# First-stage units and chunk units of a fused Fourier filter and feed-forward kernel, planned at other steps

## The chip, the cores and the metric

The kernel runs on one core of one Trainium2 chip. The metric is the device time of one execution in microseconds; the median of several executions is compared. Engines are named as in the profile: PE is TensorE's matmul, PEld its weight load, DVE is VectorE, ACT ScalarE, POOL GpSimd, SP the engine whose queue issues most DMAs.

## The reference

The input x has 8 batches of 3008 tokens with 256 channels. Each channel of each batch is filtered along the tokens in the frequency domain, and the result goes through a feed-forward layer with a hard-swish. All is fp32.

```python
X = np.fft.rfft(x, axis=1)                      # x: (8, 3008, 256)
y = np.fft.irfft(X * F[None], n=3008, axis=1)   # F = filt_r + 1j * filt_i, (1505, 256)
h = y.reshape(24064, 256) @ w_in                # w_in: (256, 2048)
g = h * np.clip(h + 3.0, 0.0, 6.0) / 6.0
out = g @ w_out                                 # w_out: (2048, 256)
```

## The kernel before

**The feed-forward is the main loop.** The 24064 tokens are 47 blocks of 512 (index k), and the 2048 hidden columns are 8 parts of 256 (index p). One step of the loop is one pair (k, p), numbered 8k + p. It multiplies up with w_in (`up_1` to `up_5`, L570, into the PSUM tiles `al` and `be`), applies the hard-swish on ACT and DVE (L615, L620), and multiplies down the part before it with w_out (`down`, L646, into four PSUM banks `po`). Both products use seven half-size products each in place of eight (Strassen's scheme), with the sums on DVE (L627 to L630) and, for the up side, on POOL (`t_sums`, L563). The sums of a finished block are added up, and its output stored, in the first two steps of the block after (`out_1` to `out_5`, stores on SP at L723).

**The Fourier filter of later batches is planned into the steps of the loop.** 3008 is 47 x 64, and the transform is split accordingly. For one batch it is a chain of units:

- `a_unit` (L385), eight per batch, the first stage: 16 matmuls from four loaded columns of x (ring `xs` of three) into two PSUM banks of the pool `psF`. ACT evicts the first bank into a tile of `t1p` (L388), and `a_sums` on DVE (L394, L395) combines it with the second bank, which is read straight from PSUM and stays taken until then. `z_store` (L402) writes the tile to HBM with four DMAs on POOL's queue. `x_load` (L322) loads the columns on SP.
- `t2_load`, `b_unit` (L428), `f_unit` (L449 to L451), `y_unit` (L459, L460): the second stage and the filter itself.
- `bi_unit` (L471), six per batch, the first inverse stage: four products into two banks of `psF`, both evicted by ACT (L474), then `g_store` on POOL's queue (L491).
- `t4_load` (L517, on SP) and `n_unit` (L524), the last inverse stage: each chunk of up to five columns of 94 tokens has two halves, dh = 0 and dh = 1, each with one bank of `psF` and an eviction by ACT into `xn` (L530), the feed-forward's input. The half that completes a block starts `t_sums`.

The pool `psF` has two banks, and all of these units share them. The pool `t1p` has two tiles.

**What sets the order.** A dictionary `plan` maps a step to functions, filled by `at(step, fn, ...)`. Functions listed in `EARLY` (`a_unit`, `b_unit`, `bi_unit`, `n_unit`) run in a step right after `up_1`, so their matmuls stand behind its three products on PE; all others run at the end of the step. Within a step they run in the order in which they were planned: chunk units first, then batch by batch. The queues of all engines are in program order.

For batch index n from 2 to 7 `places(n)` gives the steps. With `first[n]` the first block that holds tokens of the batch (0, 5, 11, 17, 23, 29, 35, 41), the eight first-stage units stand in the two blocks from step 8 x first[n] - 56 on, here called the batch's window; "+1" is the window's second step. The inverse units of a batch stand at 8 x first[n] - 40 + 16r + (8, 14, 17) for r = 0 and 1. The chunk units stand by a table `N_AT` of kinds of block, one letter for each block of the window and the four that follow; its entries are the steps of the two halves for a chunk that is alone in its block, for the first of two and for the second of two. A chunk that begins a batch and is alone in its block has both halves at +6.

```python
for n in range(2, B):
    for d, kind in enumerate("aaABAB"):
        kinds[first[n] - 7 + d] = kind
...
if c >= 3:
    at(max(a_at[c - 3], s - 6), x_load, n, c)
```

Of the kernel before, what the change touches and what calls it, by code (L numbers as in the profile page):

```python
# [33 lines left out]
B = 8  # L34
# [11 lines left out]
NP = DFF // 256  # L46
# [90 lines left out]
def kernel(  # L137
# [365 lines left out]
    def token(i):  # L503
        b, j, n = chunks[i]
        return b * N + j * TOK, n * TOK
# [230 lines left out]
    with tc.manual_schedule():  # L736
# [112 lines left out]
        n_at = {0: -2, 1: -2}  # L849
        kinds = {}  # L850
        for n in range(2, B):
            for d, kind in enumerate("aaABAB"):
                kinds[first[n] - 7 + d] = kind

        N_AT = {"a": ((2, 4), (2, 4), (6, 6)), "A": ((4, 5), (1, 1), (4, 5)), "B": ((2, 3), (1, 1), (2, 3))}
        N_FIRST = {0: ((3, 4),), 1: ((), (2, 2), (3, 3)), 2: ((1, 1),), 3: ((1, 1),)}
        in_block = {}
        for i in range(2, len(chunks)):
# [2 lines left out]
        for i in range(2, len(chunks)):  # L861
            k = token(i)[0] // BLK
            head = chunks[i][1] == 0
            same = in_block[k]
            steps = (N_FIRST.get(k - 1) or N_AT[kinds.get(k - 1, "a")])[same.index(i) + 1 if len(same) > 1 else 0]
            if head and len(same) == 1:
# [12 lines left out]
        def places(n):  # L879
            if n == 1:  # L880
                return (list(range(2, NB + 2)), [12, 13, 15, 18, 19, 20, 22, 23, 26, 27, 28, 30],
                        [14, 15, 16, 19, 21, 22, 24, 25, 27, 29, 30, 31], [16, 21, 24, 29, 31, 32])
            k = first[n] * NP
            a_at = [k - 7 * NP + i for i in (1, 3, 5, 7, 9, 11, 13, 15)]
            f_at, y_at, bi_at = ([k - (5 - 2 * r) * NP + i for r in range(2) for i in p]
                                 for p in ((2, 3, 6, 7, 12, 13), (4, 5, 10, 11, 14, 15), (8, 14, 17)))
            return a_at, f_at, y_at, bi_at

        prev = None
        for n in range(1, B):  # L890
            a_at, f_at, y_at, bi_at = places(n)
            for c, s in enumerate(a_at):
                at(s, a_unit, n, c)
                if n > 1:
                    at(s, a_sums, n, c)
                at(s, z_store, n, c, nc.sync if n == 1 else nc.gpsimd)
                if c >= 3:
                    at(max(a_at[c - 3], s - 6), x_load, n, c)
                elif n > 1:
                    at(max(prev[c + NB - 3], s - 6), x_load, n, c)  # L900
            for c in range(NT):
                s = f_at[2 * (c - TB) + (n == 1)] + 1 if c >= TB else a_at[-1] + 1
                at(s, t2_load, n, c)
                s = f_at[2 * (c - FB) + 1] + 1 if c >= FB else a_at[-1 if n > 1 else 3] + 1
                at(s, table_load, n, c)
            for i in range(NU):
                if i % 2 == 0 or n == 1:
                    at(f_at[i], b_unit, n, i)
                if i % 2 == 0:
                    at(bi_at[i // 2], bi_unit, n, i)  # L910
                    at(bi_at[i // 2], g_store, n, i)
                at(y_at[i], y_unit, n, i)
            for i in range(NU):
                at(f_at[i], f_unit, n, i)
            prev = a_at
# [4 lines left out]
        for i in range(len(items) + 1):  # L920
            up = i < len(items)
            k, p = items[min(i, len(items) - 1)]
# [54 lines left out]
        k, v, add = NBLK - 1, nc.vector.tensor_tensor, ALU.add  # L977
# [37 lines left out]
```

## Time and profile before

The five runs have a median of 2712.89 us (2712.3 to 2714.12). The profiled execution took 2712.89 us, with a span of 2711.1 us from the first to the last recorded instruction.

| engine | busy us | instructions |
|---|---|---|
| ACT | 1308.1 | 2614 |
| POOL | 373.2 | 598 |
| DVE | 2022.8 | 3503 |

| group | busy us | one, ns |
|---|---|---|
| PE, down products, L646 | 1402.8 | 276 |
| PE, first stage, L385 | 65.0 | 389 |
| PE, inverse stage, L471 (batch index 1 to 7) | 51.8 | 614 |
| PE, last inverse stage, L524 | 124.5 | 272 |
| ACT, eviction of the inverse stage, L474 | 53.0 | 595 |
| ACT, eviction of the first stage, L388 | 37.5 | 598 |

A group is all instructions of one source line on one engine. Matmuls of fp32 appear as two instructions each. Their ends are modelled and they overlap, so the length of a step is read from the start of a matmul to the start of the same matmul one step later, not from busy times. A wait in the list of waits names the engine and line that waited, who released it, the total in microseconds, how often, and the longest. The chain of waits follows the last instruction back to what released it, step by step.

### The profile page before, as it was taken

How to read it: one execution, taken by the hardware profiler on the slowest of the kernel's cores; microseconds unless marked ns; L12 is line 12 of the kernel's file. 1: busy time of each engine (PE TensorE's matmuls, PEld its weight loads, DVE VectorE, ACT ScalarE, POOL GpSimd, SP SyncE). 2: the span in 40 equal slices, each digit the busy share in tenths (PEclk: the TensorE clock that was granted, in tenths of full speed). 3: DMA queues.
4: the chain of work that ended last, by engine and by line, in shares of the span. 5: the costliest groups of instructions: out<-in, count | busy, mean ns of one | idle time of the engine just before them, and what ended most of it. 6: DMA issues, size and time to landing. Idle time of an engine off the chain costs nothing.

```text
span 2711.1 us, 48871 instructions
## 1 busy us (share of the span) xinstructions
PE 2679.5 (99%) x18846; PEld 2368.8 (87%) x18846; DVE 2022.8 (75%) x3503; ACT 1308.1 (48%) x2614; POOL 373.2 (14%) x598
## 2 busy tenths in 40 slices
PE   9899999999999999999999999999999999999998
PEld 6588889888898888888898888888888988899997
DVE  7968867787677876787767877678776778766665
ACT  3344444444444444444454544445444454444443
POOL 2421111101110012100121011210112101000000
PEclk9999999999999999999999999999999999999999
DMA  8732133211332123321233112331123321110000
GB/s 234 206 104 72 50 87 93 73 35 45 86 96 70 35 50 93 90 63 36 51 98 90 55 38 53 94 90 55 37 55 93 90 58 36 42 31 17 18 9 16
DMA packets 106597, 185.88 MB, mean 69 GB/s; under 512 B 23609, under 2 KB 66297, under 8 KB 106049
## 3 DMA queue, kind: packets, MB, share of 16 engines
q1 hardware_dynamic: 88607, 138.05, 18.1%
q0 software_dynamic: 17152, 44.22, 6.2%
q8 instruction: 149, 2.44, 0.4%
q14 instruction: 83, 0.68, 0.1%
q10 hardware_dynamic: 606, 0.49, 0.1%
HBM read 110.74 MB, written 71.93 MB: 67 GB/s over the span
## 4 chain that ended last, share of the span: by engine, by line
PE 96%; DVE 3%; ACT 0%; DMA 0%; issue 0%; POOL 0%; POOLq 0%; DVEq 0%; SPq 0%
PE po L646 43%; PE al L570 24%; PE be L570 17%; PE psn L524 4%; PE psf L471 2%; PE psf L385 2%; PE psf L428 1%; PE po L352 1%; PE po L437 0%; PE psf L437 0%; DVE g L620 0%; DVE y L277 0%; DVE y L288 0%; DVE y L290 0%; DVE w_all L293 0%; PE al L779 0%
## 5 line engine op out<-in xcount | busy, mean ns | idle before, releaser
L646 PEld LDWEIGHTS po<-w_all,g 128*128 128x128 f32 x10304 | 1363.3, 191 | 145.4 <-issue 35.0
L646 PE MATMUL po<-w_all,g 128*128 128x128 f32 x10304 | 1402.8, 276 | 0.6 <-DVE g L620 0.6
L615 ACT ACTIVATE r<-h,half_c 128x512 f32<-128x512 f32 x736 | 531.3, 722 | 328.4 <-DVE h L596 316.4
L620 DVE SCALAR_TENSOR_TENSOR g<-r,h 128x512 f32<-128x512 f32 x736 | 506.6, 688 | 208.7 <-ACT r L615 194.4
L570 PE MATMUL al<-xt,w_all 128*128 128x256 f32 x2208 | 660.0, 381 | 1.2 <-DVE h L601 0.6
L570 PE MATMUL be<-xn,w_all 128*128 128x256 f32 x1472 | 437.8, 379 | 0.0
L596 DVE TENSOR_TENSOR h<-be,s 128x512 f32<-128x512 f32 x368 | 254.3, 691 | 224.2 <-PE be L570 213.4
L570 PEld LDWEIGHTS al<-xt,w_all 128*128 128x128 f32 x2208 | 335.2, 192 | 2.5 <-issue 1.3
L570 PEld LDWEIGHTS be<-xn,w_all 128*128 128x128 f32 x1472 | 279.7, 190 | 37.9
L610 ACT ACTIVATE h<-al 128x256 f32<-128x256 f32 x368 | 141.4, 384 | 344.2 <-PE al L570 344.2
L601 DVE TENSOR_TENSOR h<-al,s 128x256 f32<-128x256 f32 x368 | 156.2, 424 | 166.9 <-PE al L570 165.8
L628 DVE TENSOR_TENSOR g<-g 128x512 f32<-128x512 f32 x368 | 255.9, 695 | 12.6
L591 ACT ACTIVATE s<-al 128x256 f32<-128x256 f32 x368 | 141.4, 384 | 208.4 <-PE al L570 206.2
L582 ACT ACTIVATE s<-be 128x256 f32<-128x256 f32 x368 | 141.4, 384 | 176.3 <-PE be L570 176.3
L570 PE MATMUL al<-xn,w_all 128*128 128x256 f32 x736 | 219.9, 381 | 0.5 <-ACT h L610 0.5
L570 PE MATMUL be<-xt,w_all 128*128 128x256 f32 x736 | 218.9, 379 | 0.0
L630 DVE TENSOR_TENSOR g<-g 128x256 f32<-128x256 f32 x368 | 170.8, 464 | 12.5
L581 ACT ACTIVATE s<-al 128x256 f32<-128x256 f32 x368 | 141.4, 384 | 70.9 <-PE al L570 70.9
L627 DVE TENSOR_TENSOR g<-g 128x256 f32<-128x256 f32 x368 | 156.6, 426 | 12.6
L402 POOL DMA_DIRECT2D z_tmp<-t x192 | 95.5, 504 | 457.2 <-DVE t L395 447.1
L570 PEld LDWEIGHTS be<-xt,w_all 128*128 128x128 f32 x736 | 139.8, 190 | 18.9
L491 POOL DMA_DIRECT2D g_tmp<-t x84 | 52.9, 634 | 580.2 <-ACT t L474 580.2
(139 smaller groups left out, 1832.8 us busy)
## 6 DMA issues: line engine op xcount, KB each, us to landing
g_tmp<-t POOLq DMA_DIRECT2D x96, 256.0 KB, 3.7
t<-g_tmp SPq DMA_DIRECT2D x188, 120.0 KB
t<-z_tmp SPq DMA_DIRECT2D x42, 512.0 KB
z_tmp<-t POOLq DMA_DIRECT2D x192, 96.0 KB, 4.0
out_dram<-o SPq DMA_DIRECT2D x321, 47.0 KB
xs<-in_x_dram SPq DMA_DIRECT2D x112, 128.0 KB
ft<-in_filt_r_dram SPq DMA_DIRECT2D x168, 64.0 KB
ft<-in_filt_i_dram SPq DMA_DIRECT2D x168, 64.0 KB
```

The lines of the kernel that those rows point to most:

```text
L570: nc.tensor.matmul(ps, w_in[p][:, w, :], x, start=start, stop=stop, skip_group_check=True)
L581: nc.scalar.activation(out=s[:, 0, :], in_=al, func=AXT.Copy)
L582: nc.scalar.activation(out=s5, in_=be[:, 1, :], func=AXT.Copy)
L591: nc.scalar.activation(out=s[:, 1, :], in_=al, func=AXT.Copy)
L596: nc.vector.tensor_tensor(out=st["h"][0].rearrange("p (a n) -> p a n", a=2), in0=be, in1=s, op=ALU.add)
L601: nc.vector.tensor_tensor(out=st["h"][1][:, 256:512], in0=al, in1=s5, op=ALU.add)
L615: nc.scalar.activation(out=r, in_=st["h"][i], func=AXT.Relu, bias=half_c, scale=1.0 / 6.0)
L620: nc.vector.scalar_tensor_tensor(out=st["g", k, p][:, o:o + 2, :].rearrange("p a n -> p (a n)"), in0=st["r", i], scalar=1.0, in1=st["h"][i ...
L627: v.tensor_tensor(out=g[:, G1, :], in0=g[:, G3, :], in1=g[:, G22, :], op=ALU.add)
L628: v.tensor_tensor(out=g[:, G3:G2 + 1:2, :], in0=g[:, G3:G1 + 1, :], in1=g[:, G11:G11 + 1, :].broadcast_to([P, 2, 256]), op=ALU.subtract)
L630: v.tensor_tensor(out=g[:, G4, :], in0=g[:, G12, :], in1=g[:, G2, :], op=ALU.subtract)
L646: nc.tensor.matmul(st["po", k][bank][:, part, u, :], g[:, a, ts(u, P)], w_out[p][:, w, :], start=(p == 0 and n in OPENS and u == 0), stop= ...
```

## The change

Two lists of steps change. In the window's first block (new kind "c") a chunk that is alone has both halves at +6, the first of two chunks both halves at +3, and the second both at +6; before, that block was of kind "a". The eight first-stage units stand at +2, +4, +7, +9, +11, +13, +14 and +15 of the window; before, at +1, +3, and so on by twos to +15. What is planned relative to these (`a_sums`, `z_store`, `x_load`, `t4_load`) moves with them. The start of `t2_load`, one step after the last first-stage unit, stays.

```diff
         for n in range(2, B):
-            for d, kind in enumerate("aaABAB"):
+            for d, kind in enumerate("caABAB"):
                 kinds[first[n] - 7 + d] = kind
 
-        N_AT = {"a": ((2, 4), (2, 4), (6, 6)), "A": ((4, 5), (1, 1), (4, 5)), "B": ((2, 3), (1, 1), (2, 3))}
+        N_AT = {"c": ((6, 6), (3, 3), (6, 6)), "a": ((2, 4), (2, 4), (6, 6)), "A": ((4, 5), (1, 1), (4, 5)), "B": ((2, 3), (1, 1), (2, 3))}
...
             k = first[n] * NP
-            a_at = [k - 7 * NP + i for i in (1, 3, 5, 7, 9, 11, 13, 15)]
+            a_at = [k - 7 * NP + i for i in (2, 4, 7, 9, 11, 13, 14, 15)]
```

The units planned into the window of batch index 3 (steps 80 to 95; the halves of a chunk are written .0 and .1, with the number of its columns):

| step | before | after |
|---|---|---|
| +1 | last inverse unit of index 2, first-stage unit 0 | last inverse unit of index 2 |
| +2 | chunk of 2, .0 | first-stage 0 |
| +3 | first-stage 1 | chunk of 2, .0 and .1 |
| +4 | chunk of 2, .1 | first-stage 1 |
| +5 | first-stage 2 | |
| +6 | chunk of 5, .0 and .1 | chunk of 5, .0 and .1 |
| +7 | first-stage 3 | first-stage 2 |
| +9 | first-stage 4 | first-stage 3 |
| +10 | chunk of 5, .0 | chunk of 5, .0 |
| +11 | first-stage 5 | first-stage 4 |
| +12 | chunk of 5, .1 | chunk of 5, .1 |
| +13 | first-stage 6 | first-stage 5 |
| +14 | | first-stage 6 |
| +15 | first-stage 7 | first-stage 7 |

The windows of indices 4 to 6 have the same list. That of index 2 has a chunk of one column and no inverse unit at +1; that of index 7 has no chunk at +2 to +4.

## Prediction, made before the changed kernel ran

> **What bounds the kernel now.** I read the busy shares, the chain that ended last, the list of waits of PE, the chain in time order around one changed place, and last the busy time of the engines step by step. A step is one pass of the main loop (256 of the 2048 hidden columns for one block of 512 tokens, with whatever is planned into it); it starts with the first product of `up_1`, the matmul `al<-xn` that follows a run of `po`.
>
> ```profile
> PE 2679.5 (99%) x18846; PEld 2368.8 (87%) x18846; DVE 2022.8 (75%) x3503; ACT 1308.1 (48%) x2614; POOL 373.2 (14%) x598
> ...
> PE 96%; DVE 3%; ACT 0%; DMA 0%; issue 0%; POOL 0%; POOLq 0%; DVEq 0%; SPq 0%
> ```
>
> TensorE sets the end: 96% of the chain is its own work. Moving a planned unit to another step neither adds nor removes a matmul, so the change can only act on the few places where PE waits. The waits of PE name one group of them:
>
> ```profile
> PE psf L385 <- ACT t L474: 3.4, 5, 0.7
> ```
>
> Five times the first-stage unit (L385) waited for the evictions of an inverse unit (L474). L385 takes two PSUM banks of tag f, L471 takes two, and the pool has two. The chain in time order at the first of the five:
>
> ```profile
> 664.52 0.86 PE be L570 x4
> 665.38 1.03 PE psf L471 x8
> 666.41 0.02 issue
> 666.43 0.61 ACT t L474
> 667.04 0.04 issue
> 667.08 1.58 PE psf L385 x16
> 668.66 0.64 PE po L646 x4
> ...
> 681.60 1.02 PE psf L385 x16
> ```
>
> The reader is to see the 0.67 us between the two units, and that the sixteen L385 matmuls then take 1.58 us against 1.02 us at 681.60, since half of them need the second bank, whose eviction runs 0.6 us behind the first. The same step and three neighbours as windows (columns: stretch, length, busy time of PE, PEld, DVE, ACT, POOL, granted clock, DMA share and rate):
>
> ```profile
> 663.92:673.54 9.62, 8.94 (x68) 6.60 (x67) 6.10 (x14) 4.66 (x10) 1.92 (x3) 1.00 0.23 60
> 888.79:896.15 7.36, 7.36 (x52) 5.91 (x51) 5.42 (x12) 4.05 (x9) 1.93 (x3) 1.00 0.26 62
> 723.38:730.75 7.37, 7.37 (x61) 6.22 (x60) 6.04 (x14) 3.58 (x8) 0.73 (x1) 1.00 0.01 3
> 717.23:723.38 6.15, 6.15 (x45) 5.79 (x44) 4.83 (x9) 3.46 (x8) 2.00 (x4) 1.00 0.25 65
> ```
>
> In this order: inverse unit and first-stage unit in one step, inverse unit alone, first-stage unit alone, nothing. All have the full clock.
>
> **The change, part by part.** Its own time is 2712.89 us, span 2711.1, 1.8 us outside the span; the median of the runs is also 2712.89, so differences carry over as they are.
>
> *First unit from +1 to +2 of its window.* Step +1 keeps the inverse unit alone (7.36), the unit makes some other step 7.37 in place of 6.15. Before: 9.62 + 6.15 = 15.77. After: 7.36 + 7.37 = 14.73. The gain is 1.04 us a place. Places: the window of batch index n starts at step 8 x first[n] - 56; the batch ahead has its last inverse unit at 8 x first[n-1] - 24 + 17, and first grows by 6, so that is the window's +1 for n = 3 to 7. For n = 2 the batch ahead has its own list, whose last inverse unit is at step 32, one before that window's +1. So five, as the list of waits counts, not six: 5 x 1.04 = 5.2 us.
>
> Here a rule gives another sum. Taking PE's busy row as its work, the double step has 9.62 - 8.94 = 0.68 us idle, and five of them 3.4 us. The Trainium skill's page "Trainium Kernel Development and Optimization", section Performance Expectations, says matmul busy time is a bad measure of closeness to the limit, since matmuls are pipelined, and points to weight loads. The rows side with it: the L385 group counts 1.58 us as busy for work that takes 1.02. PEld idles 9.62 - 6.60 = 3.02 us there, against 1.15 to 1.45 in the two single steps. I take 5.2, and 3.4 as its lower end; no upper end beyond 6.2 (six places) is in sight.
>
> *The other units,* from 3, 5, 7, 9, 11, 13, 15 to 4, 7, 9, 11, 13, 14, 15. In the trace such a unit costs 7.37 - 6.15 = 1.22 us at every position, so moving it is nothing on PE, provided its resources are free. New are three units in consecutive steps (+13, +14, +15), six windows. The rows of such a stretch (unit at +13 in a step that starts at 752.64; nothing at +14 from 760.01; unit at +15 from 766.16):
>
> ```profile
> 759.65 0.69 DVE L395 TENSOR_TENSOR t<-t,psf 128x512 f32<-128x512 f32 x1
> 760.01 0.60 PE L570 MATMUL al<-xn,w_all 128*128 128x256 f32 x2
> 761.34 1.50 POOL L402 DMA_DIRECT2D z_tmp<-t  x3 [0.19 <-issue]
> 768.70 0.60 ACT L388 ACTIVATE t<-psf 128x512 f32<-128x512 f32 x1 [0.65 <-PE psf L385]
> ...
> L402 POOL DMA_DIRECT2D z_tmp<-t x4: 501/506/513, 760.6 to 762.3; - x4
> DMA to landing us min/median/max: 2.3/2.4/2.5
> ```
>
> (1) PSUM: the unit's second bank is held until its `a_sums` end, 760.34, which is 0.33 us into the next step. A unit's first matmul comes 1.39 us into its step (754.03 in a step from 752.64). Slack 1.06 us: no wait. DVE keeps up: a unit's step has 4.91 to 6.04 us of DVE work in 7.37. (2) The `t1` buffers: +15 writes the buffer of +13. That store is issued by 762.84 and landed by about 765.3, 12.7 us after its step's start. The eviction at +15 comes at 768.70, and 1.22 us later once +14 holds a unit, so 17.3 us after: slack 4.6 us. Were it late, ScalarE would stand, and behind it s and r of the feed-forward, and with them PE.
>
> A rule speaks against that. The Trainium skill's page "SBUF — State Buffer", section "A bandwidth-pool intuition that's wrong (but worth ruling out)", has a GpSimd-issued DMA of 620 ns take 3100 beside a VectorE copy, because the shared port is locked. By that price four stores take 12.4 us in place of 2.0; +13 would land about 23 us after its step's start (8.0 + 12.4 + 2.5), 5.6 us too late, and six windows would lose 34 us. The row decides: beside L620, L627 and L628 of DVE, all running in those 2 us, the four took 501 to 513 ns. I take no wait. POOL's other work keeps its order: the sums at L563 still follow the store of the unit at +11, and +14 finds POOL idle but for +13's store.
>
> (3) Loads of x: the most crowded is the one after the block's 15 output stores, issued on SP from 745.08 to 748.56 because they stand ahead of it. Today it feeds +15; now the load in that place feeds +14, from about 761, 12 us later. Landing of these loads is not shown; a 512 KB load of t (issued 779.53) was used at 787.22 with no PE wait, so under 7.7 us, and this one is smaller. The first three loads just move one or two steps later with their units. I take no cost.
>
> *Chunk units.* In the window's first block the two halves of the small chunk move from +2 and +4 to one step, +3. Halves of a chunk of five cost 7.26 each in steps of their own and 8.38 together: 8.38 + 6.15 - 2 x 7.26 = 0.01. Between zero and that; I take zero. Their evictions on ACT (0.33 us each) go with them, ahead of L591, as in that doubled step. The next chunk's t4 load goes out one step earlier on SP, four issues of 4.5 us at the most, ahead of an x load that has four steps: nothing. The POOL sums for the next block are triggered by the later chunk at +6, which stays.
>
> Sum: 2712.89 - 5.2 = 2707.7, span about 2705.9.
>
> **Rivals.** *The wait moves along (no change).* The unit at +2 could meet the inverse unit's banks, or the paired chunk the unit's. For: all share two banks. Against: the evictions at +1 end by 667.6, five microseconds ahead of the next place for a unit, and the doubled chunk at +6 follows a unit today at 8.38, with no wait. To give back 5 x 1.04 would need such a meeting in every window: 2712.9. *Only PE's visible idle comes back:* 3.4 us, 2709.5. *The consecutive units collide (slower).* At +14 and +15 the unit needs a bank that the one before releases only after its sums. If DVE ended them more than 1.06 us later than now, PE would wait; at 1.06 + 0.94 = 2.0 us later each meeting would cost what the present one does beyond its two units' own (9.62 - 6.15 - 1.31 - 1.22 = 0.94, with 1.31 for an inverse unit elsewhere). Twelve meetings: 11.3 us, less 5.2 gained: 2719.0. It turns the sign from 5.2 / 12 = 0.43 us each. For it: the smallest slack of all that I found. Against: the sums' place in DVE's queue, behind L620, is the same in every step, and +13 and +14 bring DVE no more work than a lone unit's step has.
>
> **How the numbers follow.** All five go and nothing comes: 0.80, 2707.7, own range 2706.5 to 2709. Only visible idle: 0.07. Wait moves: 0.06. Collision: 0.07. A measurement of this kernel can tell about 0.2%, 5.4 us, from no change; that line, 2707.5, lies only a quarter of a microsecond under my forecast. Of the first case I give 0.34 to the far side and 0.46 to the near; with the second and third the same holds 0.59, slower 0.07. The range 2706.3 to 2710.5 holds the first two cases.
>
> **What would show it.** Right: the five waits of L385 for L474 gone from PE's list; the step of the last inverse unit 7.37 us, its follower with the unit 7.37, the paired small chunk 7.04; three steps of 7.37 in a row at +13 to +15; span near 2705.9. Wrong: L385 waiting for L395 or L474 at +14 or +15, L388 waiting for a store of z, PE waiting for xs, or an inverse step that stays above 7.5.

## The result and the profile after

| | before | changed |
|---|---|---|
| median of all runs, us | 2713.5 (44 runs) | 2708.41 (24 runs) |
| profiled execution: span, us | 2711.1 | 2706.8 |
| ratio of times | | 0.9979, interval 0.9974 to 0.9985 |

The changed kernel is 0.21% faster, about 5 us, forecast 5.2. PE's list of waits for the changed kernel begins like this; the wait of L385 for L474 was second in it before and is now nowhere in it. The first row and the others belong to the stretch ahead of step 8.

```profile
PE al L657 <- DVE g L620: 8.5, 4, 3.1
PE al L779 <- ACT r L773: 2.9, 1, 2.9
PE psn L552 <- DMA xs<-in_x_dram: 1.5, 1, 1.5
PE psn L545 <- ACT t L474: 1.0, 1, 1.0
```

The chain in time order at the place of the first meeting: the two units now stand a step apart, and each takes 1.02 us (start, length, what).

```profile
666.37 1.02 PE psf L471 x8
667.39 0.64 PE po L646 x4
...
672.88 0.86 PE be L570 x4
673.74 1.02 PE psf L385 x16
```

The steps of the window of batch index 3, as windows of the changed kernel (columns as in the prediction): +1 with the inverse unit alone, +2 with the first-stage unit, +3 with the paired chunk halves, then +13, +14 and +15 with a first-stage unit each.

```profile
664.91:672.28 7.37, 7.37 (x53) 5.92 (x51) 5.50 (x12) 4.07 (x9) 1.93 (x3) 1.00 0.26 60
672.28:679.65 7.37, 7.37 (x61) 6.22 (x59) 4.91 (x9) 3.58 (x8) 0.00 (x0) 1.00 0.19 50
679.65:686.69 7.04, 7.04 (x53) 6.68 (x51) 4.28 (x8) 3.64 (x9) 2.02 (x4) 1.00 0.48 132
751.38:758.75 7.37, 7.37 (x61) 6.22 (x59) 4.91 (x9) 3.58 (x8) 0.00 (x0) 1.00 0.23 69
758.75:766.12 7.37, 7.37 (x61) 6.22 (x59) 5.24 (x10) 3.58 (x8) 1.99 (x4) 1.00 0.21 56
766.12:773.49 7.37, 7.37 (x61) 6.22 (x59) 5.23 (x10) 3.58 (x8) 1.98 (x4) 1.00 0.21 55
```

Every step has its forecast length. Summed over the sixteen steps of each window, after less before is -0.09 us for batch index 2 and -1.04 us for each of 3 to 7.

**A finer measure than the time.** I took the start of the first product of every step from the traces. From step 8 (the first with `up_1`) to the last step, called the loop below, the kernel before takes 2547.61 us and the changed one 2542.33: 5.28 less. The tail behind it differs by 0.02 us. The stretch ahead of it, the same program in both, took 141.55 and 142.63 us, which is why the spans differ by only 4.2. Over all profiled executions here that stretch took 140.46 to 145.79 us (the last section says what went with it). It hides differences of a microsecond in single runs, and steps of the loop show them. All loop figures below come from one profiled execution each.

### The profile page after: what moved, and what is told of

It reads as the page before. It is cut to its first block, busy times and chain, and to the rows that moved or that the text cites. A ratio compares the mean times of both kernels' runs of the same rounds, so it can differ in the third digit from the quotient of the medians.

```text
span 2706.8 us, 48891 instructions
## 1 busy us (share of the span) xinstructions
PE 2677.1 (99%) x18846; PEld 2366.8 (87%) x18846; DVE 2024.0 (75%) x3503; ACT 1307.8 (48%) x2614; POOL 373.9 (14%) x598
## 4 chain that ended last, share of the span: by engine, by line
PE 96%; DVE 3%; DMA 0%; issue 0%; ACT 0%; POOL 0%; SPq 0%; POOLq 0%; DVEq 0%
PE po L646 43%; PE al L570 24%; PE be L570 18%; PE psn L524 4%; PE psf L471 2%; PE psf L385 2%; PE psf L428 1%; PE po L352 1%; PE po L437 0%; PE psf L437 0%; DVE g L620 0%; DVE y L288 0%; DVE y L277 0%; DVE y L290 0%; DVE w_all L293 0%; PE al L779 0%
## 5 line engine op out<-in xcount | busy, mean ns | idle before, releaser
L596 DVE TENSOR_TENSOR h<-be,s 128x512 f32<-128x512 f32 x368 | 254.2, 691 | 221.9 <-PE be L570 210.0
L601 DVE TENSOR_TENSOR h<-al,s 128x256 f32<-128x256 f32 x368 | 156.2, 424 | 165.9 <-PE al L570 164.8
L563 POOL TENSOR_TENSOR xt<-xn 128x256 f32<-128x256 f32 x92 | 68.8, 747 | 473.8 <-ACT xn L530 453.5
```

What stands on the lines that cost most here:

```text
L596: nc.vector.tensor_tensor(out=st["h"][0].rearrange("p (a n) -> p a n", a=2), in0=be, in1=s, op=ALU.add)
L601: nc.vector.tensor_tensor(out=st["h"][1][:, 256:512], in0=al, in1=s5, op=ALU.add)
```

## Experiments

My theory: the whole gain is five meetings of two two-bank units in the two banks of `psF`; the rest of the change is neutral and serves to keep new meetings from arising. The rivals: the rest of the change brings or costs something; consecutive units are coupled; or it is the step with p = 1, with its output sums, that wants relief.

| run | ratio to before, interval | loop, us | loop less the changed kernel's |
|---|---|---|---|
| changed | 0.9979 (0.9974 to 0.9985) | 2542.33 | |
| unit_back | 1.0001 (0.9992 to 1.0009) | 2548.10 | +5.77 |
| no_pair | 1.0001 (0.9992 to 1.0010) | 2546.81 | +4.48 |
| unit_at_0 | 1.0003 (0.9994 to 1.0012) | 2547.94 | +5.61 |
| unit_at_0_free | 0.9988 (0.9979 to 0.9997) | 2544.69 | +2.36 |
| inverse_later | 0.9988 (0.9979 to 0.9997) | 2544.57 | +2.24 |
| chunks_at_0 | 0.9979 (0.9970 to 0.9988) | 2541.69 | -0.64 |
| sums_late1 | 0.9977 (0.9967 to 0.9987) | 2542.32 | -0.01 |
| sums_late3 | 1.0028 (1.0019 to 1.0037) | 2555.97 | +13.64 |
| one_t1 | 1.0128 (1.0113 to 1.0143) | 2582.99 | +40.66 |

### The first unit back beside the inverse unit

```diff
-            a_at = [k - 7 * NP + i for i in (2, 4, 7, 9, 11, 13, 14, 15)]
+            a_at = [k - 7 * NP + i for i in (1, 4, 7, 9, 11, 13, 14, 15)]
```

> The changed kernel with its first first-stage unit put back to +1; the other seven units and the paired chunk halves stay as changed. My theory: the five meetings return, 9.62 us each, and the rest of the change is worth nothing; same as before within 0.5 us, step lengths elsewhere as in the changed kernel. Rival (the rest of the change brings or costs something by itself): a difference from before of 1 us or more.

Measured: the time before. In each of the five windows the sum of the steps is that of the kernel before within 0.01 us, with 9.62 us at +1. The window of index 2, without a meeting, is 0.52 us longer than before, in the step of its doubled chunk (8.99 for 8.47). The chain there runs through the chunk's load (`DMA t<-g_tmp`), which ends at 365.5, 1.7 us into the step; the chunk's matmuls start only then. In the changed kernel the same step has no wait and takes 8.38 us. So one unit's step carries the gain; the other seven units and the paired chunk bring nothing by themselves, and in this order they cost 0.52 us at one late load.

### The first unit at +0: an expectation that failed

```diff
# the kernel before
-            a_at = [k - 7 * NP + i for i in (1, 3, 5, 7, 9, 11, 13, 15)]
+            a_at = [k - 7 * NP + i for i in (0, 3, 5, 7, 9, 11, 13, 15)]
```

> The kernel before with one number changed: the first first-stage unit of each window at +0 in place of +1; all other units and chunk units as before. My theory (the whole gain is the meeting of the inverse unit and the first-stage unit in the two banks of psF): the five meetings at +1 go, 5 x 1.04 = 5.2 us, and one new one comes at step 32, where the window of batch index 2 puts its first unit beside the last inverse unit of batch index 1, about 1.0 us; 4.2 us faster than before, steps +1 at 7.37 us and step 32 at about 9.5 us. Rival (the gain comes from the paired chunks or the consecutive units, or from taking work out of the step with p = 1 in general): less than 2 us.

Measured: no gain at all, where 4.2 us were expected. The five steps at +1 take 8.25 and four times 8.00 us, not 7.37, and the steps 32 and 33 of the window of index 2 cost 2.2 us together, not 1.0. Chain and DVE's timeline of this run, at +1 of index 3 (a step from 671.52):

```profile
672.98 1.90 PE psf L471 x8
```

```profile
670.98 0.68 DVE L691 TENSOR_TENSOR o<-po,p 128x512 f32<-128x512 f32 x1
671.77 0.42 DVE L696 TENSOR_TENSOR o<-po,o 128x256 f32<-128x256 f32 x1
672.34 0.69 DVE L394 TENSOR_TENSOR t<-t,psf 128x512 f32<-128x512 f32 x1
673.06 0.69 DVE L395 TENSOR_TENSOR t<-t,psf 128x512 f32<-128x512 f32 x1
```

The unit stands alone at +0, a step with p = 0, where DVE does the output's sums L691 and L696 ahead of `a_sums`. The unit's sums then end at 673.75, 2.2 us into the next step, where elsewhere they end 0.33 us into it. The inverse unit there needs that bank, and its matmuls take 1.90 us in place of 1.02. My theory had to be widened: a first-stage unit holds its second bank until its sums, so the step after it counts too, and how far depends on what DVE has at that p.

### The same, with the bank freed early

```diff
# unit_at_0
+        second = ps[1]
+        if b > 1 and c == 0:
+            second = sp.tile([P, 512], FP32, name="s1").rearrange("p (j d) -> p j d", d=D)
+            nc.scalar.activation(out=second, in_=ps[1], func=AXT.Copy)
-        st["t1", b, c] = t, ps[1]
+        st["t1", b, c] = t, second
```

> The first unit at +0 as in unit_at_0, but ScalarE evicts that unit's second bank too (into a tile of the filter products' pool), and a_sums takes it from there, so the bank is free about 3.8 us into the step and not only after the sums. My theory (the 0.63 to 0.88 us that the inverse unit at +1 lost there were its wait for the bank that L395 still read): that step at 7.37 us in the five windows, 3.3 us faster than unit_at_0; the surplus of steps 32 and 33 stays; about 3 us faster than before. Rival (VectorE's lateness after a step with p = 0 holds up PE in any case, by the down products, whoever holds the bank): the step stays at 8.0 us or more.

Measured: the loop is 3.25 us shorter than in unit_at_0, and 0.12% faster than before. Four of the five steps are at 7.37 us, the one at index 3 at 7.56; the excess of steps 32 and 33 stayed. The extra eviction and the inverse unit in this run's chain and ACT's timeline (lines behind the edit are 4 higher):

```profile
662.69 0.59 ACT L392 ACTIVATE s<-psf 128x512 f32<-128x512 f32 x1
```

```profile
668.49 1.02 PE psf L475 x8
...
671.91 0.43 PE al L574 x2
672.34 1.05 PE po L650 x8
673.40 0.47 PE al L574 x2
```

DVE ends the unit's sums just as late as in unit_at_0 (669.27, again 2.2 us into the step), but PE no longer cares: it was the bank. What is left at index 3, the 1.05 us of eight `po` matmuls that take 0.89 elsewhere, lies in the down products three microseconds later. There the weight load (PEld) waits 0.3 us for the output's sum on DVE (L705 in this run), which reads a `po` bank; only there is DVE's lateness itself on the path. The rival that the step with p = 1 wants relief fails as well: in the window of index 2 the kernel before has a first-stage unit alone at +1, and that step takes 7.37 us.

### A chunk half beside a unit

```diff
-            for d, kind in enumerate("caABAB"):
+            for d, kind in enumerate("aaABAB"):
```

> The changed kernel with the window's first block back at kind a, so that the halves of the small chunk stand at +2 and +4 beside a first-stage unit each, three banks of psF in one step. My theory: the unit's second bank is the one the chunk half has just filled, and its eviction on ACT (about 0.33 us, behind L582) ends some 0.5 us after the unit's first matmul; about 0.5 us in each of ten steps, 5 us slower than the changed kernel, so about the time before. Rival (the chunk rows of the table are there for order only and a chunk half beside a unit costs nothing): the time of the changed kernel.

Measured: the loop is 4.48 us longer, 0.45 us for each of the ten chunk halves beside a unit. At index 3 these steps take 8.27 us, where a unit alone costs 7.37 and a chunk half adds 0.45 to an empty step. At +2 of index 3 the chain of this run shows the chunk half and then the unit's sixteen matmuls at 1.50 us instead of 1.02:

```profile
673.37 0.42 PE psn L524 x4
673.78 1.50 PE psf L385 x16
```

So the new rows of the table are no gain, but without them the units at +2 and +4 would have given back most of it. No run moves the first unit alone to +2. It would meet one chunk half there in the windows of indices 2 to 6, so by this price about 2.2 us of the gain would be lost (an estimate, 5 x 0.45).

### Consecutive units: how much slack there is

```diff
         nc.vector.tensor_tensor(out=t[:, :, 1, :], in0=t[:, :, 0, :], in1=ps, op=ALU.subtract)
+        for again in range(1 if b > 1 and c in (5, 6) else 0):     # 3 in sums_late3
+            nc.vector.tensor_tensor(out=t[:, :, 1, :], in0=t[:, :, 0, :], in1=ps, op=ALU.subtract)
```

> The changed kernel with the first VectorE operation of a_sums done twice for the units at +13 and +14 of each window, which ends the sums 0.68 us later; the result is the same. My theory (a consecutive unit waits for its second bank only when the sums end later than 1.06 us after their present end): slack of 0.38 us left, no wait, the time of the changed kernel within 0.5 us. Rival (the slack is smaller than read, the semaphore's way to PE being part of it): up to 12 x 0.3 = 4 us slower.

> The changed kernel with the first VectorE operation of a_sums done four times for the units at +13 and +14 of each window, which ends the sums 2.0 us later; the result is the same. My theory: past the slack of 1.06 us, so L385 at +14 and +15 waits about 1.0 us each for L395, 12 x 1.0 = 12 us slower than the changed kernel, and somewhat more since L620, L627 and L628 behind the sums hold up the down products. Rival (the bank isn't what couples consecutive units): no L385 wait for L395, and a loss, if any, in L646 alone.

Measured: with one repetition every step has the changed kernel's length (loop 0.01 us different). With three, the steps +14 and +15 take 8.52 for 7.37 us in all six windows, 12 x 1.15 = 13.8 us, and PE's list of waits has a new second row (lines are 2 higher behind the edit):

```profile
PE psf L385 <- DVE t L397: 6.1, 12, 0.5
```

Twelve meetings, as in the rival that forecast a loss. The chain in time order at +14 of index 3 goes from the sums straight to the unit's matmuls, 14 of its 16:

```profile
760.63 0.70 DVE t L397
761.32 0.04 issue
761.37 1.09 PE psf L385 x14
```

The list shows 0.5 us of the 1.15 us of each. The sums at +13 end 1.05 us into the next step with one repetition and 2.50 us with three, against 0.33 in the changed kernel, so 0.72 and 2.17 us later. The slack lies between these two. If the step loses one for one past it, it is 2.17 - 1.15 = 1.02 us, where 1.06 was read from the trace.

### One buffer for the stores

```diff
-    t1p = pool("t1p", 2)
+    t1p = pool("t1p", 1)
```

> The changed kernel with one t1 tile in place of two. My theory: the unit at +14 evicts about 9.9 us after the start of +13, whose stores have landed by 12.7 us; ACT waits about 2.5 us for the landing, likewise at +15, and PE behind it up to that: 12 meetings x up to 2.5 us = 20 to 30 us slower in the windows, nothing at units two steps apart (17.1 us), and some more in the first batches, where units are in consecutive steps too. Rival (the store's landing is far earlier, or ACT's wait is hidden by its idle time): under 5 us in the windows.

Measured: 16.6 us in the six windows (0.8 to 1.0 us at +14, 1.2 to 4.1 at +15), 24.2 us in steps 8 to 10, nothing at units two steps apart. Part of this is the clock: at the longest waits TensorE's granted clock is at half (0.50 in 151.5 to 158.1 us and 168.6 to 185.4, in steps 8 to 10, and in 1475.9 to 1479.1, at the end of the one step that lost 4.1). ACT's timeline at +14 of index 3 and PE's list:

```profile
791.36 0.60 ACT L388 ACTIVATE t<-psf 128x512 f32<-128x512 f32 x1 [2.80 <-DMA z_tmp<-t]
```

```profile
PE al L570 <- ACT s L591: 31.1, 14, 13.4
```

ACT waited 2.80 us for the landing, near the 2.5 us expected, and the step lost 0.98 us of it; the remainder was time in which ACT would have idled (in the changed kernel's next step it idles 0.65 us ahead of this eviction and 0.46 behind it). The expectation of 20 to 30 us in the windows was too high for that reason. With two tiles the wait is not there.

### Two attempts at a better version

```diff
# inverse_later
-                                 for p in ((2, 3, 6, 7, 12, 13), (4, 5, 10, 11, 14, 15), (8, 14, 17)))
+                                 for p in ((2, 3, 6, 7, 12, 13), (4, 5, 10, 11, 14, 15), (9, 15, 17)))
# and in N_AT: "A": ((4, 5), (0, 0), (4, 5)), "B": ((2, 3), (0, 0), (2, 3))
```

> The changed kernel with the first two inverse units of each half-batch one step later (+9 and +15 in place of +8 and +14), and the paired chunks of kinds A and B at +0 in place of +1, so that none stands beside an inverse unit. In the changed kernel an inverse unit costs 1.31 us at the old places and 1.22 us at p = 1, since the second bank is still read by L451 of the step before; 24 places x 0.09 = 2.2 us, and the step with a chunk pair and an inverse unit loses its surplus of 0.6 us. My theory (every wait for a psF bank is worth its length and nothing else bounds the step): 2.8 us faster than the changed kernel, 8 us faster than before. Rival (at p = 1 and p = 7 the output's sums on DVE make the inverse unit as dear, or g_store lands too late for the chunk's load): no gain over the changed kernel, or a loss.

Measured: 2.24 us longer than the changed kernel. The inverse units did become cheaper, 7.37 us in place of 7.46. But the step that each of them left follows an `f_unit`, and 23 of these 24 steps, with no unit's matmul in them, take 6.34 to 6.43 us, where an empty step elsewhere takes 6.15. Together that is 5.2 us, against about 2.1 gained at the inverse units and 0.8 at the two moved pairs of chunk halves. The windows of steps 72 and 73, one inverse unit's place and the one after it, in this run (first) and in the changed kernel:

```profile
603.53:609.93 6.40, 6.38 (x44) 5.85 (x43) 5.75 (x11) 3.58 (x8) 0.00 (x0) 1.00 0.01 3
609.93:617.30 7.37, 7.37 (x52) 5.92 (x51) 5.48 (x12) 4.07 (x9) 1.92 (x3) 1.00 0.26 60
```

```profile
603.50:610.96 7.46, 7.46 (x52) 6.01 (x51) 5.92 (x11) 4.56 (x10) 1.25 (x2) 1.00 0.28 68
610.96:617.11 6.15, 6.15 (x44) 5.79 (x43) 5.37 (x12) 2.98 (x7) 0.73 (x1) 1.00 0.03 12
```

In the emptied step DVE has 5.75 us of work, among it the filter product L451 of the step before, and PE has only 6.15 us to hide it. DVE's timeline shows which side is late: in the changed kernel L596 waits for PE, in this run it starts at once.

```profile
607.69 0.69 DVE L596 TENSOR_TENSOR h<-be,s 128x512 f32<-128x512 f32 x1 [0.38 <-PE be L570]
```

```profile
607.37 0.69 DVE L596 TENSOR_TENSOR h<-be,s 128x512 f32<-128x512 f32 x1
```

PE's last `al` product of the step then starts at 608.54, right after DVE's L601, which reads `al` until 608.39, and its two matmuls take 0.67 us in place of 0.43. That PE waits for DVE here is read from these times; its list of waits does not show it, and no run moved DVE's work. If it is so, the inverse unit, with its 0.09 us of waiting, had covered 0.19 to 0.28 us of another wait. My expectation had left out what the unit covers.

```diff
# chunks_at_0, from the changed kernel
-"A": ((4, 5), (1, 1), (4, 5))
+"A": ((4, 5), (0, 0), (4, 5))
```

> The changed kernel with one entry of the table moved: the pair of chunk halves of kind A from +1 to +0, which takes the pair at step 257 out of the step with an inverse unit (10.28 us for it and 6.15 for the empty step ahead). My theory: 8.38 + 7.37 in their place, 0.68 us faster than the changed kernel and nothing else; 6 us faster than before. Rival (the pair at p = 0 delays the inverse unit at p = 1 as the first-stage unit did): no gain.

Measured: steps 256 and 257 take 8.38 and 7.37 us for 6.15 and 10.28, and the loop is 0.64 us shorter, the shortest of all. The ratio, 0.9979, can't be told from that of the changed kernel.

## Why the prediction was right

- **The meetings.** Five, worth 1.04 us each by the windows' sums; forecast 1.04. That the window of index 2 has none is confirmed: it changed by 0.09 us, at its doubled chunk, which the forecast did not have; its cause was not followed.
- **The rule on busy time.** The 3.4 us that PE's busy row allowed was wrong and 5.2 right. What the list of waits shows (0.68 us a meeting) is the wait ahead of the first matmul; the rest lies between matmuls that are counted as one busy group. sums_late3 shows the same: 0.5 of 1.15 us.
- **The consecutive units.** No wait. The sums at +13 end at 759.08, 0.33 us into the next step, as read before. The +14 step's store issues are 498 to 511 ns each beside two-input VectorE work, so the 3100 ns of the rule that spoke against it did not come; this run's stores of +13 have landed by 763.2, and the eviction at +15 comes at 768.65, 17.3 us into +13's step as worked out.
- **The chunk halves.** 7.04 us for the pair as forecast, neutral in sum. What the prediction did not price is that they must move: 0.45 us a step otherwise. It put the chunks' loads at nothing without working out when they land. That held in the changed kernel, but unit_back lost 0.52 us at one of them, so on this point it was luck.
- **The rival that failed, and a reason that did.** Against the collision the prediction said that the sums' place in DVE's queue is the same in every step. unit_at_0 shows that this holds only away from p = 0, where the output's sums go ahead of them and the step after loses 0.63 to 0.88 us to the same unit. The changed list has no unit at p = 0; the forecast stood because of that, not because of the reason given.
- **The bound.** The forecast put the time within 0.2% with 0.59 and beyond with 0.34. It measured 0.21%, with an interval on both sides of the line; the loop's 5.28 us is 0.19%. The chances were as undecided as the result.

## What to carry to other kernels

In this kernel, with PE 99% busy, what could still be gained lay in pairs of tasks that want the same few buffers in the same step. In such a case count the buffers that each task holds and until when, and price a meeting by the length of the whole step against steps with one task each, since a busy row hides the part of the wait that falls between matmuls. A buffer's holder is its last reader, so look also at the step after, and at what else that reader's engine does there. Before moving a task out of a step, ask which lateness of another engine it was covering.

## What was not expected of the hardware

Nearly all steps of the loop repeat to 0.01 us between executions: sums_late1 and the changed kernel differ by 0.01 us over 367 steps. (One step, 241, took 0.13 us less in two of the other runs.) The stretch of some 141 us ahead of the loop, the same program every time but for one_t1, varied by 5.3 us between profiled executions.

The traces show two parts of that, in the ten runs without one_t1. The first up product of block 0 (L657) starts at 67.2 to 70.3 us. From there to step 8 seven runs take 73.20 to 73.25 us, the changed kernel and inverse_later 74.92, and unit_at_0 75.53. The second part goes with TensorE's granted clock. It falls to half for 3.4 us or more in every run: from 120 to 123 us on in the seven (0.50 in 121.5 to 124.7 us of the kernel before), from 133 us on in the two (0.50 in 133.5 to 136.7 of the changed kernel), and twice in unit_at_0, which also has 0.50 in 68.2 to 74.8 us. So the changed kernel's profiled execution lost 1.7 us ahead of the loop that are not the change's. Why the clock falls at one place or the other was not tried, and whether the spread of the whole time comes from this stretch alone is not shown, since each kernel has one profiled execution.
